# Attention scores in halves of 288 keys, with the high-by-high product on two halves of TensorE's rows

## The chip, the cores and the metric

The kernel runs on one core of a Trainium2 chip. What counts is the device time of one execution in microseconds (us); the median of three runs is given beside their lowest and highest.

## What is computed

Attention with a learned bias on relative positions for 4 batches, 8 heads, 576 positions and 64 values a head, then a mixture of 8 experts on its output, whose gate is balanced in 8 rounds of row and column sums. The change stands in the scores of the attention:

```python
scores = scale * np.matmul(q, k.transpose(0, 1, 3, 2))      # 4 x 8 heads, 576 x 576
bias = np.maximum(x @ w1 + b1, 0.0) @ w2                    # x from relative positions
scores = scores + bias.transpose(2, 0, 1)[None]
scores = scores - np.max(scores, axis=-1, keepdims=True)
attn = np.exp(scores)
attn = attn / (np.sum(attn, axis=-1, keepdims=True) + 1e-09)
out = np.matmul(attn, v)                                     # then experts: relu(x @ w1[e]) @ w2[e]
```

Inputs are float32. The kernel splits each operand into a high and a low float16 part and adds the products of parts that matter.

## The kernel before

**Stages.** Up to about 150 us the bias tables are built, expert by expert weights are loaded and the largest values of q, k and v are found. The attention runs beside this from 67 us and alone with expert 0 from about 205 to 490 us. Then come the gate, the rest of expert 0 and, to the end, experts 1 to 7.

**Units and tiles.** A unit is a pair of heads of one batch, 16 in all. `u_trans` (line 747) turns the parts of q and k so that the 64 values of a head lie on partitions: 18 transposes on TensorE into the PSUM tile `l`, and three copies out of it into `qkT`, the first and third on ScalarE, the second (k) on VectorE. `qkT` holds for q and for k the high part on partitions 0 to 63 and the low part on 64 to 127. Two copies on GpSimd (`pairs`, line 727) then make a third block in which q's low part is on partitions 0 to 63 and its high part on 64 to 127.

**Scores.** `scores` (line 898) makes one tile of 128 queries by 576 keys in the PSUM tile `s`, which spans two banks of 512 columns. For both blocks of q (as stored, and turned) it multiplies all 128 partitions with 512 keys and then with 64 keys: high by high plus low by low from the first, low by high plus high by low from the second. That is four matmuls a tile. For t = 4 the tile takes 64 queries of each of the two heads, one head on each half of the output partitions, and has eight matmuls of half the width. There are 9 tiles a unit, 144 in all. The keys stand in the order that the bias tables were built for.

**After the scores.** `st_max` (line 922) adds the bias and finds the row's extreme in one VectorE pass (`sb`, a custom operation that reads `s`); ScalarE takes the exponential, VectorE the reciprocal, ScalarE and VectorE write the high and low part `ah`, a transfer on SyncE's queue turns it into `aT` (line 981), and `attend` (line 983) multiplies with v into the tile `pv`, one head on each half of the output partitions; one pair of its 14 pairs of matmuls has only 64 partitions of input.

**What sets the order.** All of this is recorded as nodes with a cost and sorted by a planner (`Plan.emit`, line 131): each engine takes, of the nodes whose inputs are ready by the estimated times, the one of highest urgency. The cost of a TensorE node is given by `cost` (line 227): for an output of over 64 partitions, at least 64 or the width, divided by 2350, in us. Matmuls of expert 0 are nodes of the lowest urgency (`run_piece`, line 868); they fill TensorE between scores and `pv` groups and write the PSUM tile `l` too. A step is two tiles (or the one tile of t = 4), 5 steps a unit; the scores of a step are recorded one step ahead, and `u_trans` of unit u (from the fourth on) at step 5u - 4, its first scores at 5u - 1. All recorded instructions carry line 211, so the trace is read by tile names.

Of the kernel before, what the change touches and what calls it, by code (L numbers as in the profile page):

```python
# [18 lines left out]
P = 128  # L19
B, H, S, D = 4, 8, 576, 64  # L20
# [5 lines left out]
R = S // 64  # L26
# [163 lines left out]
class Engine:  # L190
# [36 lines left out]
    def cost(self, op, out, ins):  # L227

        n = max(x.free_size() for x in [out] + ins)
        columns = sum(x.free_size() == 1 for x in ins)  # L230
        if self.name == "pe":
            c = 4 if ins[0].dtype == F32 else 1
            if out.partition_size() > 64:
                return c * max(64, out.free_size()) / 2350
            return c * max(82, out.free_size()) / 3500
        if self.name == "act":
            return (0.13 if ins and ins[0].space == PSUM else 0.16) + 0.03 * columns + n * 0.00097
        if self.name == "pool":
            return 0.15 + n * 0.0016
        if op == "tensor_copy" and ins[0].dtype == out.dtype == F16:  # L240
            return 0.06 + n * 0.00027
        if n <= 2:
            return 0.08
        return 0.12 + n * (0.0012 if ins[0].space != PSUM else 0.00112)
# [27 lines left out]
def attention_sinkhorn_moe(ctx, tc, q, k, v, w1, b1, w2, wg, m1, m2, xm, xm4, xf, sel, out):  # L272
# [141 lines left out]
    with ExitStack() as actx:  # L414
# [105 lines left out]
        for kind in range(1, 4):  # L520
            vec.scalar_tensor_tensor(
                out=wr,
# [101 lines left out]
        def bias_step(between=()):  # L624
# [33 lines left out]
            out=w2m,  # L658
# [68 lines left out]
        def pairs(o, i):  # L727
            pool.tensor_copy(o.bitcast(U32), i.bitcast(U32))
# [18 lines left out]
        def u_trans(u):  # L747
            if u >= len(units):
                return
            st = U[u]  # L750
            if u in (2, 3):
                qkT = xc[:, u - 2, : 27 * P].rearrange("p (n x) -> p n x", x=P)
            else:
                qkT = uni.tile([P, 27, P], F16, name="qkT", tag="qkT")
            qk = st.pop("qk").rearrange("p (i r) a d -> p i r (a d)", i=2)
            for i in range(3):
                ps = psA.tile([P, 1024], F16, name="ps_t", tag="l1", bufs=2).rearrange("p (r x) -> p r x", x=P)
                rows = [(i, r) for r in range(8)] if i < 2 else [(0, 8), (1, 8)]
                with plan.as_one():
                    for j, (a, r) in enumerate(rows):  # L760
                        pe.transpose(ps[:, j], qk[:, a, r], id16)
                if i == 0:
                    act.copy(
                        qkT[:, 0:8].rearrange("p (h t) (i x) -> p h t i x", h=2, i=2),
                        ps.rearrange("p (i t) (h x) -> p h t i x", i=2, h=2),
                    )
                elif i == 1:
                    vec.tensor_copy(qkT[:, R : R + 8], ps)
                else:
                    act.copy(qkT[:, : 2 * R].rearrange("p (i r) x -> p i r x", i=2)[:, :, 8], ps[:, 0:2])  # L770
            for i in range(2):
                pairs(qkT[64 * i : 64 * i + 64, 2 * R :], qkT[64 - 64 * i : 128 - 64 * i, :R])
            kv = qkT[:, R : 2 * R + 1].rearrange("p (r c) x -> p c r x", r=2)
            st.update(q=(qkT[:, :R], qkT[:, 2 * R :]), kT=qkT[:, R : 2 * R], kv=kv)

        def b_load(u, hh):

# [7 lines left out]
        def b_tile(u, t, hh):  # L785
            if t in (2, 3):
                return U[u]["b", hh][:, t - 2, :]
            hp = units[u][1]
            return br[t][:, 2 * hp + hh, :] if t < 2 else br4[:, hp, :]
# [107 lines left out]

        def scores(u, t, hh):
            ps = ps_s()
            kT = U[u]["kT"]  # L900
            kv = U[u]["kv"]
            for a, qT in enumerate(U[u]["q"]):
                for c in range(2):
                    for h in (hh,) if t < 4 else (0, 1):
                        hs = slice(h * 64, h * 64 + 64)
                        lhs = qT[:, 4 * h + t, :] if t < 4 else qT[:, 8, hs]
                        rhs = kT[:, 4, hs] if c else kv[:, :4, :, hs]
                        o = (ps if t < 4 else ps[hs])[:, 512 * c : 512 + 64 * c]
                        pe.matmul(o, lhs, rhs, start=(a == 0), stop=(a == 1))
            return ps  # L910

# [10 lines left out]
        def st_max(s):  # L922
            u, gi, hh = s["key"]
            st = wrk.tile([P, 4, 2], F32, name="st", tag="st", bufs=5)
            s["st"], s["sb"] = st, []
            for i, t in enumerate(s["ts"]):
                sb = wrk.tile([P, S], F32, name="sb", tag="sb", bufs=6)
                s["sb"].append(sb)
                vec.tensor_tensor_reduce(
                    out=sb,  # L930
                    in0=s["ps"][i][:, :S],
                    in1=b_tile(u, t, hh),
                    scale=nc8[:, 0:1],
                    scalar=3.0e38,
                    op0=ALU.add,
                    op1=ALU.min,
                    accum_out=st[:, 0, i : i + 1],
                )
# [1058 lines left out]
```

## Time and profile before

| | us |
|---|---|
| median of three runs | 1743.61 (1743.52 to 1743.78) |
| the profiled execution | 1743.0 |
| its span, first to last instruction | 1741.2 |
| mean granted clock of TensorE | 0.984 |

The profile is of one execution. Engines: PE is TensorE's matmuls, PEld its weight loads, DVE VectorE, ACT ScalarE, POOL GpSimd, SP SyncE. A matmul's row gives start and length; matmuls overlap, so the spacing of starts tells the rate and not the length. `128*64` behind the tiles is the used part of the array, rows by columns. A busy share over the whole span mixes stages with different limits, so it is read by stage.

### The profile page before, as it was taken

How to read it: one execution, taken by the hardware profiler on the slowest of the kernel's cores; microseconds unless marked ns; L12 is line 12 of the kernel's file. 1: busy time of each engine (PE TensorE's matmuls, PEld its weight loads, DVE VectorE, ACT ScalarE, POOL GpSimd, SP SyncE). 2: the span in 40 equal slices, each digit the busy share in tenths (PEclk: the TensorE clock that was granted, in tenths of full speed). 3: DMA queues.
4: the chain of work that ended last, by engine and by line, in shares of the span. 5: the costliest groups of instructions: out<-in, count | busy, mean ns of one | idle time of the engine just before them, and what ended most of it. 6: DMA issues, size and time to landing. Idle time of an engine off the chain costs nothing.

```text
span 1741.2 us, 40333 instructions
## 1 busy us (share of the span) xinstructions
PE 1667.7 (96%) x16596; PEld 1368.3 (79%) x16596; DVE 1440.8 (83%) x2622; ACT 1070.2 (61%) x1906; POOL 96.8 (6%) x137
## 2 busy tenths in 40 slices
PE   7887897999999999999999999999999999999998
PEld 4554564656585888888988898889888888888887
DVE  7998989898869999787878887988788878876666
ACT  7897888888857655456455545555555644443443
POOL 0102011111002310000000000000000000000000
PEclk9988898999999999999999999999999999999999
DMA  7869899999976446734664555456544743463321
GB/s 256 257 172 235 190 211 208 215 203 208 185 228 212 148 164 230 247 145 147 218 231 170 174 187 212 173 177 237 208 163 158 281 155 133 181 224 99 102 76 37
DMA packets 291965, 324.61 MB, mean 186 GB/s; under 512 B 183100, under 2 KB 217412, under 8 KB 286788
## 3 DMA queue, kind: packets, MB, share of 16 engines
q1 hardware_dynamic: 291780, 322.04, 61.0%
q8 instruction: 129, 2.11, 0.5%
q14 instruction: 56, 0.46, 0.1%
HBM read 191.43 MB, written 88.08 MB: 161 GB/s over the span
## 4 chain that ended last, share of the span: by engine, by line
PE 81%; DVE 9%; DMA 4%; ACT 3%; issue 2%; POOL 0%; SPq 0%; DVEq 0%; ACTq 0%; POOLq 0%
PE bankA L1608 18%; PE bankA L1628 14%; PE bankE L1628 9%; PE bankB L1628 9%; PE bankE L1608 9%; PE l L211 7%; PE s L211 5%; PE bankB L1608 4%; PE pv L211 3%; DMA aT<-ah 2%; ACT area L211 1%; DVE area L211 1%; DVE ah L211 1%; DMA aT<-xc 1%; PE bankB L375 1%
## 5 line engine op out<-in xcount | busy, mean ns | idle before, releaser
L1608 PEld LDWEIGHTS <-slot 128*128 128x128 f16 x5040 | 451.0, 98 | 51.1 <-issue 5.3
L1628 PEld LDWEIGHTS <-hA 128*128 128x128 f16 x2268 | 221.0, 98 | 26.6 <-DVE hA L1220 1.2
L211 PEld LDWEIGHTS <-area 128*128 128x128 f16 (+1 forms) x2477 | 153.8, 100 | 102.8 <-issue 33.1
L1608 PE MATMUL bankA<-xt,slot 128*128 128x256 f16 (+1 forms) x1680 | 186.1, 262 | 0.7 <-ACT u L1665 0.7
L1608 PE MATMUL bankE<-xt,slot 128*128 128x256 f16 (+1 forms) x1680 | 186.1, 262 | 0.3 <-DVE c L1220 0.3
L1653 ACT ACTIVATE hA<-c 128x512 f16<-128x512 f32 x189 | 118.3, 628 | 108.5 <-DVE c L1220 107.5
L1628 PEld LDWEIGHTS <-hS 128*128 128x128 f16 x1512 | 147.5, 98 | 20.2 <-DVE hS L1659 1.9
L1628 PEld LDWEIGHTS <-area 128*128 128x128 f16 x1512 | 147.7, 98 | 17.1
L1712 ACT COPY u<-bankA 128x512 f32<-128x512 f32 (+1 forms) x70 | 37.9, 541 | 178.9 <-PE bankA L1628 178.8
L1220 DVE SCALAR_TENSOR_TENSOR hA<-c,hA 128x512 f16<-128x512 f32 x189 | 128.3, 690 | 16.0 <-ACT hA L1653 13.9
L1665 ACT ACTIVATE u<-bankA 128x512 f32<-128x512 f32 x126 | 75.1, 596 | 79.0 <-PE bankA L1608 71.9
L211 PE MATMUL l<-area 128*128 128x512 f16 (+1 forms) x413 | 110.0, 384 | 5.5 <-ACT area L211 1.3
L211 ACT ACTIVATE sb<-sb,st 128x576 f32<-128x576 f32 x144 | 110.6, 770 | 7.1 <-DVE st L211 6.8
L1220 DVE SCALAR_TENSOR_TENSOR acc<-c,fs,acc 128x256 f32<-128x256 f32 x252 | 110.3, 479 | 2.0
L211 DVE SCALAR_TENSOR_TENSOR ah<-sb,st,ah 128x576 f16<-128x576 f32 x121 | 97.5, 828 | 13.4 <-ACT ah L211 13.4
L211 PE MATMUL s<-qkT 128*128 128x512 f16 (+3 forms) x560 | 83.0, 297 | 15.5 <-DVE st L211 14.4
L211 ACT ACTIVATE ah<-sb,st 128x576 f16<-128x576 f32 x121 | 89.4, 771 | 11.6 <-DMA aT<-ah 9.6
L1628 PE MATMUL bankA<-area,hS 128*128 128x256 f16 x756 | 88.9, 273 | 1.8 <-ACT hS L1653 1.0
L1628 PE MATMUL bankA<-area,hA 128*128 128x256 f16 x756 | 88.4, 273 | 1.0 <-DVE hA L1220 1.0
L1628 PE MATMUL bankB<-area 128*128 128x256 f16 x756 | 88.3, 273 | 0.0
L1628 PE MATMUL bankB<-area,hA 128*128 128x256 f16 x756 | 88.3, 273 | 0.0
L1628 PE MATMUL bankA<-area 128*128 128x256 f16 x756 | 88.3, 273 | 0.0
(248 smaller groups left out, 3166.7 us busy)
## 6 DMA issues: line engine op xcount, KB each, us to landing
sc_w<-stage SPq DMA_DIRECT2D x84, 512.0 KB
acc<-sc_y SPq DMA_DIRECT2D x102, 256.0 KB
area<-sc_w SPq DMA_DIRECT2D x48, 512.0 KB
sc_y<-acc SPq DMA_DIRECT2D x84, 256.0 KB
xt<-sc_t SPq DMA_DIRECT2D x20, 1024.0 KB
slot<-sc_w SPq DMA_DIRECT2D x36, 512.0 KB
bt<-sc_bias SPq DMA_DIRECT2D x26, 576.0 KB
raw<-in_moe_w_dram SPq DMA_DIRECT2D x28, 512.0 KB
```

Of the source, the lines that this page charges most:

```text
L211: self.plan.record(self.name, cost, lambda: fn(*args, **kw), ins, outs, move)
L375: pe.matmul(ps, w[:, a, ft * P : (ft + 1) * P], xs(xp, dt, p0, W), start=(dt == 0 and j == 0), stop=(dt == 3 and j == 2),)
L1220: vec.scalar_tensor_tensor(out=o, in0=x, scalar=s, in1=y, op0=op0, op1=op1)
L1608: pe.matmul(ps[:, jf * w : jf * w + w], t[:, a, c * 512 + f * P : c * 512 + f * P + P], x(xp, c), start=(first and jf == 0 and c == 0 and ...
L1628: pe.matmul(ps[:, j * 256 : j * 256 + 256], h[:, a, fc * w + j * P : fc * w + j * P + P], t[:, wp, fc * 256 : fc * 256 + 256], start=(firs ...
L1653: on_act(0.58, lambda: act.activation(h[:, 0, sl], x, AF.Relu if relu else AF.Copy), [r], wk)
L1665: on_act(0.55, lambda: act.activation(tmp[k], bank[b], f, scale=HS), [b], [k], 0)
L1712: on_act(0.27 * nt, lambda: act.copy(tmp[k][:, :n], bank[b][:, :n]), [b], [k], 0)
```

## The change

`qkT` keeps its size and is laid out by head: for each head the 576 queries, and likewise the 576 keys, stand in one run (`qH`, `kH`, `zH` are views of the three blocks, two heads by 576). The copies out of `l` write in this layout. A third copy on GpSimd puts the high part of the last 288 keys of k over q's low part on partitions 64 to 127, once the turned block has been made from it.

A score tile then has two matmuls on all 128 partitions, from the turned block of q, with 288 keys each (low by high plus high by low), and two on 64 partitions, high by high: the first 288 keys from partitions 0 to 63, the last 288 from partitions 64 to 127. The product low by low is left out. Each half of the keys has a PSUM bank of its own, and VectorE's pass reads two runs of 288. The planner prices a matmul whose input has 64 partitions at its width divided by 4000.

```diff
--- before.py
+++ after.py
@@ -231,7 +231,7 @@
         if self.name == "pe":
             c = 4 if ins[0].dtype == F32 else 1
             if out.partition_size() > 64:
-                return c * max(64, out.free_size()) / 2350
+                return c * max(64, out.free_size()) / (4000 if ins[0].partition_size() == 64 else 2350)
             return c * max(82, out.free_size()) / 3500
         if self.name == "act":
             return (0.13 if ins and ins[0].space == PSUM else 0.16) + 0.03 * columns + n * 0.00097
@@ -752,26 +752,39 @@
                 qkT = xc[:, u - 2, : 27 * P].rearrange("p (n x) -> p n x", x=P)
             else:
                 qkT = uni.tile([P, 27, P], F16, name="qkT", tag="qkT")
+            qH, kH, zH = (
+                qkT[:, R * i : R * i + R].rearrange("p r x -> p (r x)").rearrange("p (h s) -> p h s", h=2)
+                for i in range(3)
+            )
             qk = st.pop("qk").rearrange("p (i r) a d -> p i r (a d)", i=2)
             for i in range(3):
                 ps = psA.tile([P, 1024], F16, name="ps_t", tag="l1", bufs=2).rearrange("p (r x) -> p r x", x=P)
-                rows = [(i, r) for r in range(8)] if i < 2 else [(0, 8), (1, 8)]
+                rows = [(0, r) for r in range(8)] if i == 0 else [(1, r) for r in (0, 5, 1, 6, 2, 7, 3, 8)]
+                if i == 2:
+                    rows = [(0, 8), (1, 4)]
                 with plan.as_one():
                     for j, (a, r) in enumerate(rows):
                         pe.transpose(ps[:, j], qk[:, a, r], id16)
                 if i == 0:
                     act.copy(
-                        qkT[:, 0:8].rearrange("p (h t) (i x) -> p h t i x", h=2, i=2),
+                        qH[:, :, : 8 * D].rearrange("p h (t i x) -> p h t i x", t=4, i=2),
                         ps.rearrange("p (i t) (h x) -> p h t i x", i=2, h=2),
                     )
                 elif i == 1:
-                    vec.tensor_copy(qkT[:, R : R + 8], ps)
+                    vec.tensor_copy(
+                        kH[:, :, : 8 * D].rearrange("p h (r x) -> p r h x", r=8),
+                        ps.rearrange("p r (h x) -> p r h x", h=2),
+                    )
                 else:
-                    act.copy(qkT[:, : 2 * R].rearrange("p (i r) x -> p i r x", i=2)[:, :, 8], ps[:, 0:2])
+                    act.copy(
+                        qkT[:, : 2 * R].rearrange("p (i r) x -> p i (r x)", i=2)
+                        .rearrange("p i (h s) -> p i h s", h=2)[:, :, :, 8 * D :],
+                        ps[:, 0:2].rearrange("p i (h x) -> p i h x", h=2),
+                    )
             for i in range(2):
                 pairs(qkT[64 * i : 64 * i + 64, 2 * R :], qkT[64 - 64 * i : 128 - 64 * i, :R])
-            kv = qkT[:, R : 2 * R + 1].rearrange("p (r c) x -> p c r x", r=2)
-            st.update(q=(qkT[:, :R], qkT[:, 2 * R :]), kT=qkT[:, R : 2 * R], kv=kv)
+            pairs(qH[64:P, :, S // 2 :], kH[0:64, :, S // 2 :])
+            st.update(q=(zH, (qH[0:64], zH[64:P])), k=(kH, (kH[0:64], qH[64:P])))
 
         def b_load(u, hh):
 
@@ -897,15 +910,14 @@
 
         def scores(u, t, hh):
             ps = ps_s()
-            kT = U[u]["kT"]
-            kv = U[u]["kv"]
-            for a, qT in enumerate(U[u]["q"]):
+            (qa, qb), (ka, kb) = U[u]["q"], U[u]["k"]
+            for a in range(2):
                 for c in range(2):
                     for h in (hh,) if t < 4 else (0, 1):
-                        hs = slice(h * 64, h * 64 + 64)
-                        lhs = qT[:, 4 * h + t, :] if t < 4 else qT[:, 8, hs]
-                        rhs = kT[:, 4, hs] if c else kv[:, :4, :, hs]
-                        o = (ps if t < 4 else ps[hs])[:, 512 * c : 512 + 64 * c]
+                        o = (ps if t < 4 else ps[h * 64 : h * 64 + 64])[:, 512 * c : 512 * c + S // 2]
+                        qT, kT = (qb[c], kb[c]) if a else (qa, ka)
+                        lhs = qT[:, h, P * t : min(P * t + P, S)]
+                        rhs = kT[:, h, S // 2 * c : S // 2 * c + S // 2]
                         pe.matmul(o, lhs, rhs, start=(a == 0), stop=(a == 1))
             return ps
 
@@ -927,9 +939,9 @@
                 sb = wrk.tile([P, S], F32, name="sb", tag="sb", bufs=6)
                 s["sb"].append(sb)
                 vec.tensor_tensor_reduce(
-                    out=sb,
-                    in0=s["ps"][i][:, :S],
-                    in1=b_tile(u, t, hh),
+                    out=sb.rearrange("p (a s) -> p a s", a=2),
+                    in0=s["ps"][i].rearrange("p (a s) -> p a s", a=2)[:, :, : S // 2],
+                    in1=b_tile(u, t, hh).rearrange("p (a s) -> p a s", a=2),
                     scale=nc8[:, 0:1],
                     scalar=3.0e38,
                     op0=ALU.add,
```

On TensorE, at the first score tile of the program (`qkT` is the turned parts of q and k, `s` the score tile, `l` the target of the transposes):

```order
 L211 MATMUL l_1_115<-id_68,qk_126 128x128
 L211 LDWEIGHTS qkT_127
-L211 MATMUL s_117<-qkT_127 128x512
+L211 MATMUL s_117<-qkT_127 128x288
 L211 LDWEIGHTS qkT_127
-L211 MATMUL s_117<-qkT_127 128x64
+L211 MATMUL s_117<-qkT_127 128x288
```

The two further matmuls of the tile change in the same way; the last two of the four are those of 64 partitions, which the order does not name. The wait for GpSimd's copies moves from the third weight load of the tile to the first, and the fourth matmul waits for the third copy.

On GpSimd, at the first units' copies within `qkT` (and `xc`, where two units keep theirs):

```order
 L211 COPY qkT_127<-qkT_127 64x576 x2
+L211 COPY qkT_127<-qkT_127 64x2x144
 L211 COPY qkT_129<-qkT_129 64x576 x2
+L211 COPY qkT_129<-qkT_129 64x2x144
 L211 COPY xc<-xc 64x576 x2
+L211 COPY xc<-xc 64x2x144
```

One copy a unit is added behind the two.

On VectorE, in the stretch where the bias still runs beside the first steps (`ISA` on `sb` is the pass over the scores, `area` and `aT_0` the bias, `ah` the low part of the weights):

```order
 L211 SCALAR_TENSOR_TENSOR vs_145<-vnat_116,sms,vs_145 128x640
+L211 ISA sb_134,st_143<-s_117,br_110,sms 128x576
+L211 ISA st_143 128x1
 L211 TENSOR_TENSOR aT_0_118<-s_119,area 128x512
-L211 ISA sb_134,st_143<-s_117,br_110,sms 128x576
-L211 ISA st_143 128x1
-L211 SCALAR_TENSOR_TENSOR area<-s_119,sms,aT_0_118 128x8x32
 L211 SCALAR_TENSOR_TENSOR qk_126<-nat_121,sms,qk_126 128x9x64
```

The planner sets the pass over a score tile ahead of a bias row; on TensorE it likewise sets fillers to other places between score tiles and `pv` groups.

## Rows read from the trace of the kernel before

**Rows 1.** The page, busy time, share of the span, instructions of each engine.
```profile
PE 1667.7 (96%) x16596; PEld 1368.3 (79%) x16596; DVE 1440.8 (83%) x2622; ACT 1070.2 (61%) x1906; POOL 96.8 (6%) x137
```

**Rows 2.** Stretches of the whole span; columns named in the first line.
```profile
core 0: us, PE busy (x) PEld busy (x) DVE busy (x) ACT busy (x) POOL busy (x), PEclk, DMA share, GB/s
...
205.00:490.00 285.00, 263.58 (x2649) 170.13 (x2644) 247.37 (x572) 241.82 (x495) 36.93 (x57) 0.98 0.98 204
...
740.00:1741.00 1001.00, 993.18 (x9561) 892.46 (x9558) 792.89 (x1288) 512.98 (x846) 0.00 (x0) 1.00 0.48 169
```

**Rows 3.** The chain of waits by line, 205 to 490 us, then 67 to 205 us.
```profile
by line: PE l L211 38.3%; PE pv L211 16.8%; PE s L211 12.0%; issue 5.8%; DMA aT<-xc 5.8%; DMA aT<-ah 4.0%; DVE ah L211 3.6%; DVE sb L211 3.3%; ACT ah L211 2.6%; DMA bt<-sc_bias 1.2%; DMA sc_y<-ys 1.0%; DVE qk L211 0.8%; DVE st L211 0.7%; DV
...
by line: PE s L211 24.8%; DMA aT<-ah 10.6%; DVE area L211 10.0%; ACT area L211 8.2%; issue 7.2%; DVE sms L211 6.2%; PE l L211 5.7%; PE pv L211 5.3%; DVE ah L211 4.8%; DVE sb L211 3.3%; DVE aT L211 3.0%; ACT sb L211 1.7%; DVE st L211 1.4%; A
```

**Rows 4.** TensorE in order of time, 309.0 to 315.3 us: start, length, tiles, count.
```profile
309.62 1.14 PE L211 MATMUL s<-qkT 128*128 128x512 f16 x8
310.60 1.48 PE L211 MATMUL l<-xb,area 128*128 128x256 f16 x12
311.91 0.65 PE L211 MATMUL s<-qkT 128*128 128x512 f16 x4
312.50 1.96 PE L211 MATMUL pv<-aT,vs 128*64 128x256 f16 x28
314.39 0.28 PE L211 MATMUL l<-id,qk 128*128 128x128 f16 x2
314.60 0.68 PE L211 MATMUL s<-qkT 128*64 128x512 f16 x8
315.22 0.28 PE L211 MATMUL l<-id,qk 128*128 128x128 f16 x2
```

**Rows 5.** The same view of short cuts: inside and around one `pv` group.
```profile
313.29 0.50 PE L211 MATMUL pv<-aT,vs 128*64 128x256 f16 x4
...
313.49 0.30 PE L211 MATMUL pv<-aT,vs 64*64 64x256 f16 x2
...
313.72 0.30 PE L211 MATMUL pv<-aT,vs 128*64 128x256 f16 x2
```

**Rows 6.** Transfer queues, 205 to 490 us: packets, MB, share of 16 engines.
```profile
q1 hardware_dynamic: 146436, 57.82, 97.4%
```

**Rows 7.** Who waited for whom, 205 to 490 us: total us, times, longest.
```profile
DVE sb L211 <- PE s L211: 9.0, 14, 1.2
PE s L211 <- DVE st L211: 8.7, 12, 1.6
...
PE pv L211 <- DMA aT<-xc: 4.3, 3, 3.5
```

**Rows 8.** Groups of instructions, 0 to 760 us: busy, mean ns, idle before.
```profile
L211 DVE CUSTOM_DVE_ANT_0 sb<-s,br,sms 128x576 f32<-128x576 f32 x80 | 63.6, 808 | 4.5 <-PE s L211 4.5
...
L211 DVE CUSTOM_DVE_ANT_0 sb<-s,bt,sms 128x576 f32<-128x576 f32 x64 | 51.4, 811 | 6.9 <-PE s L211 5.9
...
L211 DVE TENSOR_TENSOR aT<-s,area 128x512 f32<-128x512 f32 x40 | 27.5, 687 | 7.1 <-PE s L211 5.8
...
L211 DVE TENSOR_TENSOR area<-l,area 128x512 f16<-128x512 f32 x27 | 18.4, 684 | 6.2 <-ACT area L211 6.0
```

**Rows 9.** Tile `qkT`, whole span: duration ns min/median/max, first and last start.
```profile
L211 PE MATMUL s<-qkT x560: 190/318/637, 67.4 to 471.4; 128*128 128x64 f16 x75, 128*128 128x512 f16 x74, 128*64 128x64 f16 x20, 128*64 128x512 f16 x18
L211 ACT COPY qkT<-l x28: 348/685/1019, 62.7 to 449.7; 128x1024 f16<-128x1024 f16 x14, 128x256 f16<-128x256 f16 x14
L211 POOL COPY qkT<-qkT x28: 662/665/1198, 64.5 to 450.9; 64x576 uint32<-64x576 uint32 x28
L211 DVE COPY qkT<-l x14: 670/683/692, 63.9 to 448.9; 128x1024 f16<-128x1024 f16 x14
```

**Rows 10.** The group of score matmuls, 205 to 490 us.
```profile
L211 PE MATMUL s<-qkT 128*128 128x512 f16 (+1 forms) x480 | 68.0, 288 | 9.0 <-DVE st L211 8.7
```

**Rows 11.** A stretch at a lower granted clock; columns as in rows 2.
```profile
300.00:307.00 7.00, 3.67 (x28) 2.40 (x28) 5.78 (x12) 4.02 (x9) 0.00 (x0) 0.52 0.98 196
```

## The prediction

> **What bounds the kernel now.** I read the busy times first [rows 1], then the same by stage [rows 2], then the chain of waits of the two attention stretches [rows 3], then TensorE's instructions in order of time where the changed work stands [rows 4, 5]. TensorE is busy 96% of the span, but the change touches only the attention, which ends near 490 us; from 740 us on TensorE is busy 993.18 of 1001 us and nothing there changes. In the steady attention, 205 to 490 us, no engine is alone: TensorE 263.58 of 285 us, VectorE 247.37, ScalarE 241.82, and the transfer queue's packets took 97.4% of 16 engines' span [rows 2, 6]. The chain settles which of them is late most often: `l`, `pv` and `s` on TensorE are 38.3 + 16.8 + 12.0 = 67.1% of it, transfers of `aT` 9.8%, VectorE's two largest lines 6.9%. In 67 to 205 us, where the bias still runs, TensorE's three are 24.8 + 5.7 + 5.3 = 35.8% [rows 3]. So two thirds of what TensorE gains or loses per score tile after 205 us should arrive at the end, and about a third before. What TensorE waits for there is small and scattered: 8.7 us for `st` on VectorE, 4.3 us for a transposed `aT` [rows 7].
>
> **Columns saved.** A score tile streams 512 + 64 + 512 + 64 = 1152 columns. Two tiles start at 309.62 and the next work at 310.60, so one takes 0.49 us [rows 4]. Twelve matmuls of 256 columns go from 310.60 to 311.91, 0.109 us each, so one of 288 columns takes 0.109 x 288 / 256 = 0.123 us. The new tile has two of them on all 128 rows (0.245 us) and two on 64 rows. If those two run side by side they cost one, 0.123 us; that two matmuls on different parts of the array can do so is seen for the two column halves: a `pv` group has 28 matmuls of 256 columns and takes 1.89 us, where 28 one after the other would be 3.05 [rows 4]. For two row halves no row shows it. Side by side, a tile streams 0.368 us: 0.12 us saved, and 144 tiles (80 against `br`, 64 against `bt` [rows 8]) save 17.7 us of TensorE. One after the other, nothing is saved, since 4 x 288 is again 1152.
>
> **Switches added.** The price that the diff does not show is the change between matmuls that use the whole array and matmuls that use a part. It is in the trace of before, at every `pv` group. The stretch from 311.91 to 314.39 holds one score tile (0.49 us), 14 pairs (14 x 0.109 = 1.53 us) and the switches into the group, to the 64-row pair inside it, back, and out: 2.48 - 2.02 = 0.46 us for four, 0.116 us each [rows 4]. The same in single starts: pairs that otherwise follow at 0.11 us stand 0.20 us ahead of the 64x64 pair (313.29 to 313.49) and 0.23 us behind it (313.49 to 313.72) [rows 5]. That pair differs from its neighbours in rows alone, which makes it the nearest row to a change from 128 to 64 rows. With 128 columns at this type no row shows such a change; the two ends for its price are 0 (nothing drains) and 0.14 us (0.23 of the way back, less 0.09), and I take 0.116. The Trainium skill, page TensorEngine Tiling (Array Packing), section Key Properties, says that a change of tiling mode, and not of the tile alone, drains the engine; the rows just named agree, and by that rule the price stands for 64x128 too.
>
> Counted in the order of the built programs, TensorE changes its form 110 times outside the `pv` groups before and 372 times after: each of the 144 tiles has one switch more inside, and one more behind it unless a `pv` group follows at once. 262 x 0.116 = 30.4 us added against 17.7 saved: TensorE has 12.7 us more to do, 0.09 us a tile. A whole-array tile amid other whole-array work goes from 0.49 to 0.368 + 0.232 = 0.60 us; a tile before a `pv` group, and the t = 4 tile, which stands between two switches already (0.62 us from 314.60 to 315.22 [rows 4]), stay as they are.
>
> **The other parts.** Row copies: VectorE's copy of k writes runs of 64 in place of one run of 1024. It took 0.683 us, ScalarE's copies of such runs up to 1.019 [rows 9]; so 0 to 0.34 us on each of 16, at most 5.4 us on an engine whose two largest lines are 6.9% of the chain, under 0.5 us at the end. A gain is excluded, the elements being the same. I take 0. VectorE's pass over the scores reads two runs of 288; reading PSUM in runs of 32 (the bias, 687 ns for 512) costs what reading it in one run does (684 ns for 512, the fillers) [rows 8], so 0, and 144 x 0.003 = 0.4 us either way as bound. GpSimd gets one copy more a unit, of half the elements of one of 0.665 us: 16 x 0.33 to 0.67. It is busy 36.93 of 285 us [rows 2]; the first score matmul now waits for it, but the transposes are issued three steps ahead of a unit's first scores (about 14 us at 60 steps in 285 us), and the list of waits of before has no score matmul behind GpSimd [rows 7]. If that cover were gone it would cost 0.7 us a unit, 11 us in all. Only unit 0 is near: its copies start at 64.5, its scores at 67.4 [rows 9]; 0.4 us there, in a stretch where TensorE is a third of the chain. I take 0. What queues behind a late score on TensorE is the next filler or `pv` group, and what queues behind its `sb` on VectorE is the low part of the step before, whose transpose the transfer queue waits for.
>
> **The order.** The planner's price of a tile falls from 0.49 to 0.389 us while the tile by my sum rises to 0.60, so it sees room that is not there and sets expert-0 matmuls (the `l` fillers) earlier: around the 13th to 15th `pv` group up to 24 matmuls of 256 columns (2.6 us) earlier, elsewhere the same or within 12. The total is the same. Bounds for this: 2.6 us either way; I take 0.
>
> **The sum.** 12.7 us over 144 tiles. After 205 us stand 480 score matmuls [rows 10], 12 units of 40, which is 108 tiles: 9.5 us x 0.67 = 6.4 us; 36 tiles before: 3.2 x 0.36 = 1.1 us. Together 7.5 us. The profiled execution took 1743.0 us with a span of 1741.2; the median of the three runs is 0.6 above it, and the sum on the median is 1743.6 + 7.5 = 1751.
>
> **Rivals.**
> *The switch by rows alone is nearly free and the halves do run side by side.* Then 17.7 us are saved: 13.3 x 0.67 + 4.4 x 0.36 = 10.5 us less, 1733 us. For it: no row shows 128 to 64 rows at 128 columns. Against it: the 64x64 pair of [rows 5]. It decides when a switch costs under 17.7 / 262 = 0.068 us. The Trainium skill, page TensorEngine Tiling (Array Packing), section Theoretical Speedup, gives up to 2x for a side of at most 64 and charges nothing in that place, which is this case; the trace has the drain beside the gain at every `pv` group.
> *The halves run one after the other.* Each tile streams as before and the switches are all on top: 22.8 x 0.67 + 7.6 x 0.36 = 18.0 us, 1762 us. For it: no row has two row halves at work. Against it: the column halves.
> *Absorbed.* The transfers, not TensorE, set the pace from 205 to 490 us, and the added 9.5 us fill waits that TensorE has anyway (the 13 us of [rows 7] named above); then 0 to 3 us arrive, 1745 us. For it: 97.4% [rows 6]; against it: 67% against 9.8% of the chain.
> A further risk goes one way: where TensorE stood idle, its granted clock fell to its lower level, as in 300 to 307 us (0.52, with TensorE busy 3.67 of 7 us) [rows 11]. One more such stretch costs at most 3.5 us, half of its length.
>
> **Chances.** Forecast as summed (1746 to 1758) 0.54; one after the other (1758 to 1770) 0.10; absorbed (1740 to 1746) 0.22; free switches or a lucky order (1730 to 1740) 0.14. The range leaves out the last and the upper part of the second: 1740 to 1764. A difference of 0.2%, 3.5 us, is about what a measurement of this kernel can tell from none: faster 0.14, same 0.22, slower 0.64.
>
> **What would show it.** In the profile after: a score tile amid `l` work from 0.49 to about 0.60 us, its last two starts within 10 ns of each other (0.12 us apart if they queue), about 0.2 us in place of 0.12 between the second and the third start, and 0.2 us from the last start to the next whole-array matmul. TensorE's work from 205 to 490 us would stretch by some 6 us, and the stage from 740 us on would keep its length. The forecast is wrong if the third start follows the second at 0.13 us (no switch), or if the tile takes 0.60 us and the attention still ends at 490 us (absorbed).

## The result and the profile after

The changed kernel takes 1758.74 us (median of 4 runs, 1755.04 to 1759.57); the kernel before, run beside it, takes 1743.69 (1743.52 to 1743.81). The ratio is 1.0083, with an interval of 1.0068 to 1.0098. A second set of runs gave 1753.56 (5 runs, 1753.27 to 1757.39) and 1.0064 (1.0051 to 1.0076). So the change costs 0.6 to 0.8%, 11 to 15 us. I had forecast 7.5 us, with a range up to 20: slower, as forecast, and one and a half to two times as much of it. The experiments ask where the rest comes from.

The profiled execution took 1759.57 us, its span 1757.6. First the page of the changed kernel, the busy time of TensorE as in [rows 1]:

```profile
PE 1683.4 (96%) x16596; PEld 1365.0 (78%) x16596; DVE 1442.1 (82%) x2622; ACT 1070.2 (61%) x1906; POOL 105.6 (6%) x153
```

TensorE is busy 15.7 us longer with as many matmuls; VectorE and ScalarE do what they did, and GpSimd has 16 copies more (8.8 us). Where the attention ends is seen at the first matmul of the routing after it. Before, in order of time (start, length, what, tiles, count):

```profile
492.58 1.36 PE L1276 MATMUL bankS<-wgs,xa 128*128 128x8 f16 x48
```

After, the same row:

```profile
508.81 1.36 PE L1288 MATMUL bankS<-wgs,xa 128*128 128x8 f16 x48
```

It starts 16.23 us later. From there to the last matmul the two executions take 1244.5 and 1244.6 us, and each kernel run below 1243.2 to 1245.5. So the whole loss lies in the attention, and this one row tells how late a profiled execution is.

**A score tile after**, TensorE in order of time, to be laid beside [rows 4]; then the same kernel in short cuts, whose starts give the single matmuls:

```profile
332.85 0.64 PE L211 MATMUL s<-qkT 128*128 128x288 f16 x4
333.42 1.48 PE L211 MATMUL l<-xb,area 128*128 128x256 f16 x12
...
324.29 0.64 PE L211 MATMUL s<-qkT 128*128 128x288 f16 x4
324.86 0.41 PE L211 MATMUL pv<-aT,vs 128*64 128x256 f16 x4
```

```profile
332.97 0.52 PE L211 MATMUL s<-qkT 128*128 128x288 f16 x3
...
333.19 0.30 PE L211 MATMUL s<-qkT 64*128 64x288 f16 x2
333.42 0.28 PE L211 MATMUL l<-xb,area 128*128 128x256 f16 x1
```

The four starts are 332.85, 332.97, 333.19 and 333.19 (3 ns apart by the records' own times): the two halves run side by side. The third start is 0.22 us behind the second, where a matmul of 288 columns alone takes 0.123, and the next whole-array matmul 0.23 behind the pair. So a switch (the change between matmuls that use the whole array and matmuls that use 64 rows) costs about 0.10 us each way, and a tile amid whole-array work takes 0.57 us against 0.49 before. Ahead of a `pv` group (324.29 to 324.86) it takes 0.57 against 0.59 in [rows 4].

**The stages and the chain.** The stretch of [rows 2], 205 to 490 us, and the chain of waits from 205 us to the end of the attention, as in [rows 3]:

```profile
205.00:490.00 285.00, 265.08 (x2573) 160.67 (x2572) 242.77 (x563) 236.47 (x483) 44.47 (x72) 0.94 0.92 194
```

```profile
by line: PE l L211 46.9%; PE pv L211 19.1%; PE s L211 15.2%; issue 4.2%; DVE ah L211 2.8%; DVE sb L211 2.1%; DMA aT<-xc 1.8%; ACT ah L211 1.3%; ACT xc L211 0.8%; ACT sb L211 0.8%; DVE qk L211 0.8%; DVE area L211 0.7%; DVE st L211 0.6%; DVE 
```

TensorE's three lines rise from 67.1 to 81.2% of the chain, and transfers of `aT` fall from 9.8 to about 2%: VectorE, ScalarE and the transfers wait more for TensorE than before. In the list of waits, where the columns are total us, times and longest, two rows grew against [rows 7]:

```profile
DVE sb L211 <- PE s L211: 15.5, 18, 1.8
PE s L211 <- DVE st L211: 9.0, 10, 1.7
...
PE l L211 <- DVE qk L211: 6.8, 3, 2.8
...
PE s L211 <- POOL qkT L211: 0.2, 1, 0.2
```

VectorE waits for scores 15.5 us instead of 9.0. The wait of `l` (here the transposes of q and k) for VectorE's `qk` was a single one before, of 2.7 us, and is now three with 6.8. The one that I had weighed, scores behind GpSimd's copy, is 0.2 us in all. That extra wait for `qk` has nothing to do with a switch. It is a sign that TensorE's order is another.

### The profile page after: what moved, and what is told of

Its sections match the earlier page's. It is cut to its first block, busy times and chain, and to the rows that moved or that the text cites. A ratio compares the mean times of both kernels' runs of the same rounds, so it can differ in the third digit from the quotient of the medians.

```text
span 1757.6 us, 40416 instructions
## 1 busy us (share of the span) xinstructions
PE 1683.4 (96%) x16596; PEld 1365.0 (78%) x16596; DVE 1442.1 (82%) x2622; ACT 1070.2 (61%) x1906; POOL 105.6 (6%) x153
## 4 chain that ended last, share of the span: by engine, by line
PE 85%; DVE 9%; ACT 3%; issue 2%; DMA 2%; POOL 0%; SPq 0%; DVEq 0%; ACTq 0%; POOLq 0%
PE bankA L1620 18%; PE bankA L1640 14%; PE bankE L1640 9%; PE l L211 9%; PE bankB L1640 9%; PE bankE L1620 9%; PE s L211 5%; PE bankB L1620 4%; PE pv L211 4%; DVE area L211 1%; DVE sms L211 1%; ACT area L211 1%; DVE ah L211 1%; PE bankB L375 1%; DVE sb L211 1%
## 5 line engine op out<-in xcount | busy, mean ns | idle before, releaser
L211 PE MATMUL s<-qkT 128*128 128x288 f16 (+3 forms) x560 | 85.8, 309 | 13.7 <-DVE st L211 12.5
```

Of the source, the lines that this page charges most:

```text
L211: self.plan.record(self.name, cost, lambda: fn(*args, **kw), ins, outs, move)
```

## The experiments

Four things are mixed in the change: the layout (two banks, rows of 64), the halves side by side, the switches, and the order in which the planner lays TensorE's work, since the change also lowers the price of a tile there from 0.49 to 0.389 us while the tile really takes 0.57. My theory at the start: the layout and the order are nothing, the switches all. The rival: the order is worth as much as the switches.

**The price alone put back.** TensorE's order is then that of before in all but 16 of its 16,567 places, and the work is that of the change:

```diff
-                return c * max(64, out.free_size()) / (4000 if ins[0].partition_size() == 64 else 2350)
+                return c * max(64, out.free_size()) / 2350
```

> The change with one line taken back: the planner prices a 64-row matmul as every other (2350), so TensorE's order is that of before again, with the new score tiles in it. Theory 1 (the switches between 128 and 64 rows are the loss): TensorE still has 370 switches outside the pv groups against 110, about 0.09 us more a tile, so the time stays at 1752 to 1760 us. Rival 2 (the planner's lower price moved the fillers to wrong places, and that is the loss): 1742 to 1747 us.

Measured: 1748.87 us, ratio 1.0035 (1.0022 to 1.0047). About half of the loss is gone (from 1.0064 or 1.0083), with every switch in place. Its trace can be read beside that of before place by place (`...` in these extracts stands for rows left out). TensorE of this kernel in order of time; the second to fifth row answer to the first four of [rows 4]:

```profile
283.78 2.62 PE L211 MATMUL pv<-aT,vs 128*64 128x256 f16 x20
...
310.77 1.22 PE L211 MATMUL s<-qkT 128*128 128x288 f16 x8
311.92 1.48 PE L211 MATMUL l<-xb,area 128*128 128x256 f16 x12
313.24 0.64 PE L211 MATMUL s<-qkT 128*128 128x288 f16 x4
313.80 1.96 PE L211 MATMUL pv<-aT,vs 128*64 128x256 f16 x28
...
498.15 1.36 PE L1288 MATMUL bankS<-wgs,xa 128*128 128x8 f16 x48
```

In the execution before, the `pv` row stood at 283.79 too; two tiles took 0.98 us (here 311.92 - 310.77 = 1.15), and the attention ends at 498.15 where it ended at 492.58. So 5.6 us are lost in this execution, and none of them up to 284 us. Its mean granted clock is 0.978 where before has 0.984, but the loss doesn't hang on that: two other executions of this kernel, at 0.984 and 0.983, took 1748.78 and 1749.72 us.

**The layout alone.** Both products on all 128 rows, with the two banks, the copies in runs of 64 and the old price. The low by low products come back with it, as before:

```diff
-            pairs(qH[64:P, :, S // 2 :], kH[0:64, :, S // 2 :])
-            st.update(q=(zH, (qH[0:64], zH[64:P])), k=(kH, (kH[0:64], qH[64:P])))
+            st.update(q=(zH, (qH, qH)), k=(kH, (kH, kH)))
```

> The new layout, the halves of 288 keys and the two PSUM banks, but high by high (with low by low again) on all 128 rows, no third copy on GpSimd, and the old price: no row halves and no added switch. Theory 1: a tile is 4 x 0.122 = 0.49 us as before and the time is that of before, 1741 to 1747 us. Rival 3 (the copies in runs of 64 and VectorE's pass over two runs are the loss): 1750 us or more, with VectorE's copy or its score pass longer in the profile.

Measured: 1743.25 us, 1.0006 (0.9997 to 1.0015): nothing that can be told from the kernel before. TensorE's order is exactly that of before, four matmuls of 288 columns take what 512 + 64 did, and VectorE's pass keeps its 808 ns. In time order, a tile in this kernel, and its pass over the scores (busy us, mean ns, idle before):

```profile
373.17 0.65 PE L211 MATMUL s<-qkT 128*128 128x288 f16 x4
373.66 0.61 PE L211 MATMUL l<-id,qk 128*128 128x128 f16 x8
```

```profile
L211 DVE CUSTOM_DVE_ANT_0 sb<-s,br,sms 128x576 f32<-128x576 f32 x80 | 63.7, 808 | 5.0 <-PE s L211 4.8
```

**The halves on the same rows**, so that they can't run side by side, with everything else as in the change:

```diff
-            pairs(qH[64:P, :, S // 2 :], kH[0:64, :, S // 2 :])
-            st.update(q=(zH, (qH[0:64], zH[64:P])), k=(kH, (kH[0:64], qH[64:P])))
+            st.update(q=(zH, (qH[0:64], qH[0:64])), k=(kH, (kH[0:64], kH[0:64])))
```

> The change, but both halves of the keys on rows 0 to 63, so that the two 64-row matmuls of a tile have to follow each other; no third copy on GpSimd; price and switches as in the change. Theory 1 (in the change the halves run side by side): 0.12 us more a tile, 17.7 us more of TensorE, of which two thirds or more arrive: 1770 to 1778 us. Rival 4 (the halves queue in the change already): the time of the change, 1755 to 1760 us.

Measured: 1768.41 us, 1.0146 (1.013 to 1.0161). The tile, in time order:

```profile
385.62 0.76 PE L211 MATMUL s<-qkT 128*128 128x288 f16 x4
386.31 0.94 PE L211 MATMUL l<-xb,area 128*128 128x256 f16 x7
```

0.69 us, 0.12 more than in the change: what running side by side saves is a whole matmul of 288 columns.

**The order of that kernel without its work.** The layout kernel, whose tile takes 0.49 us, told that a tile takes 0.389. TensorE's order is the one of the kernel just above:

```diff
                     s["ps"].append(scores(u, t, hh))
+                    plan.group[1] = 0.3891 if t < 4 else 0.6583
```

> The kernel of e2 (all score matmuls on 128 rows, no third copy) with the change's price alone: a tile's node is set to 0.389 us (t = 4: 0.658), so that the planner orders nearly as in the change while a tile takes 0.49 us and no switch is added. Rival 2 in its strong form (the order itself costs, whatever the tile): 1749 to 1755 us. Its weak form (the order costs only where the tile is longer than the planner believes, by 0.1 us here against 0.19 in the change): 1743 to 1748 us. No effect of the price: 1741 to 1745 us.

Measured: 1748.67 us, 1.0017 (1.0006 to 1.0027). No switch is added, no column is saved, and 3 us are lost: the order is not nothing. It also prices the switches a second time. Same order, 0.49 against 0.69 us a tile: 1.0146 - 1.0017 = 0.0129, 22 us. With 0.20 us on the 118 tiles that have two switches more and about 0.1 on the other 26 (those ahead of a `pv` group and most with t = 4), TensorE has some 26 us more; so about 85% of it arrived.

**As large an error as the change makes.** The change's planner is wrong by 0.57 - 0.389 = 0.18 us a tile, the last kernel's only by 0.10. So the layout kernel again, with 0.30 for a tile of 0.49, and its opposite, a price too high by 0.09:

```diff
                     s["ps"].append(scores(u, t, hh))
+                    plan.group[1] = 0.30 if t < 4 else 0.56
```

> e2 (all score matmuls on 128 rows, a tile of 0.49 us) with a tile priced at 0.30 us (t = 4: 0.56), so that the planner is wrong by 0.19 us a tile, as it is in the change by 0.389 against 0.58. No switch is added. If the size of the error is what the order costs: 1750 to 1758 us. If the error alone does little and it takes the switches beside it: 1743 to 1750 us.

```diff
                     s["ps"].append(scores(u, t, hh))
+                    plan.group[1] = 0.58 if t < 4 else 0.658
```

> e2 with a tile priced at 0.58 us (t = 4: 0.658), 0.09 us too dear, which is the order of e7 but for some rows. If every order other than that of before costs some us: 1747 to 1752 us. If only a price that is too low costs: 1742 to 1746 us.

Measured: 1752.73 us, 1.0042 (1.0026 to 1.0058), and 1746.4 us, 1.0019 (1.001 to 1.0028). The error of the change's size costs 7 us with no switch at all; added to the 1.0035 of the switches it gives 1.0077, between the two ratios of the change. A price too high costs 3 us too, so what decides is not the sign of the error. Of the orders tried with the layout kernel's work, that of the old price has the lowest ratio, though the interval of 1.0006 reaches into those of 1.0017 and 1.0019.

Where these losses arise is read from the starts of VectorE's 144 passes over the scores. Against the layout kernel, which has the order of before and no switch, the k-th pass of a profiled execution starts later by so many us:

```
pass                      37     55     67    103    139
layout kernel, at      215.2  262.8  286.6  374.1  461.5
old price (switches)    -1.3    0.0    0.8    5.6    6.4
wrong price (order)      7.3    4.8   13.2   13.3   13.5
the change               6.1    3.2   12.9   14.4   16.9
the change once more     2.4   -0.5    7.2    9.7   10.9
old price, pair turned   2.2    3.3    3.6    6.3    6.9
smaller wrong price      0.4    0.9    2.5    7.8    6.7
```

("Wrong price" is the kernel with 0.30; its profiled execution took 1756.61 us, about 4 above its median. "Pair turned" is the old price's order with fewer switches, described below; "smaller wrong price" is the kernel with 0.389.) By the same measure the kernel before stands 0.4 to 1.6 us behind the layout kernel. In the first four rows the two causes seem to lie in different stretches: the switches cost little up to pass 67 and some 6 us behind it, the order costs up to pass 67 and nothing behind, and the change has both. The last two rows show that this is no rule. With the pair turned, half of the loss is there by pass 67. The smaller wrong price loses 5.3 us from pass 67 to 103, 3.9 of them from pass 95 on (352 to 374 us); from 350 to 376 us its granted clock is 0.87 where before has 1.00.

Up to pass 37 the loss is not steady: 6.1 us and 2.4 for one and the same kernel. From pass 37 to 67 it is: 5.9 us with the wrong price, 6.8 and 4.8 in the change, of which the kernel with the old price accounts for 2.1 by its switches. What TensorE's program holds there, counted in the order of the built programs: matmuls of expert 0 (in units of 256 columns), `pv` matmuls and transposes of q and k that stand ahead of the n-th of the 640 score matmuls, 4.4 to a pass:

```
score matmul   before, old price    the change       wrong price
170  (pass 38)   132  321  102     132  321  102    132  321  102
220  (pass 50)   228  405  112     252  405  112    240  405  112
250  (pass 56)   336  489  146     336  461  130    336  461  130
260  (pass 58)   360  489  146     336  489  138    336  489  138
280  (pass 63)   384  517  148     384  517  148    384  517  148
```

At both ends the same work has been done. Between them up to 24 matmuls of expert 0 come ahead of scores, as I had read from the order, and a `pv` group of 28, 16 transposes and 24 matmuls of expert 0 fall behind scores, which I had not. The scores are early then (the dip at pass 55), and what was put behind them is late. In the order of the smaller wrong price the `pv` group stands where it did and only 8 transposes fall behind (138 ahead of the 250th score matmul); from pass 37 to 67 that kernel lost 2.1 us. The link from these pieces to the loss is read from order and trace; no run moves them alone. The transposes start the next unit, and behind them TensorE has nothing to lay into a wait: in every one of these kernels about 36 us follow without a matmul of expert 0 (272.0 to 308.3 us before, 283.0 to 320.5 in the change). There TensorE stands waiting for VectorE. TensorE of the change, 289 to 316 us, with the idle time ahead of a row and its releaser in brackets:

```profile
289.20 1.94 PE L211 MATMUL s<-qkT 128*128 128x288 f16 x8 [1.07 <-DVE st L211]
293.34 1.89 PE L211 MATMUL l<-id,qk 128*128 128x128 f16 x16 [2.20 <-DVE qk L211]
295.16 3.48 PE L211 MATMUL pv<-aT,vs 128*64 128x256 f16 x28
...
310.62 1.37 PE L211 MATMUL s<-qkT 128*128 128x288 f16 x8 [1.72 <-DVE st L211]
314.76 1.04 PE L211 MATMUL l<-id,qk 128*128 128x128 f16 x8 [2.77 <-DVE qk L211]
315.72 3.48 PE L211 MATMUL pv<-aT,vs 128*64 128x256 f16 x28
```

The wrong-price kernel, without a switch, waits at the same two steps:

```profile
293.43 1.89 PE L211 MATMUL l<-id,qk 128*128 128x128 f16 x16 [2.08 <-DVE qk L211]
...
313.61 1.03 PE L211 MATMUL l<-id,qk 128*128 128x128 f16 x8 [2.28 <-DVE qk L211]
```

The kernel before has one such wait in its stretch, at 281.97, and the one with the old price too; their later one there is for a transposed `aT`:

```profile
281.97 1.03 PE L211 MATMUL l<-id,qk 128*128 128x128 f16 x8 [2.75 <-DVE qk L211]
...
303.33 3.42 PE L211 MATMUL pv<-aT,vs 128*64 128x256 f16 x27 [3.48 <-DMA aT<-xc]
```

So the waits of this stretch are no longer in the change than before (its idle times sum to 10.1 us, before to 11.8); the change comes to them later. The 28 matmuls of a `pv` group take 3.48 us there and 1.96 elsewhere: behind such waits the granted clock is for a time at the lower of its two levels (1.2 and 2.4 GHz). From 284 to 320 us its mean is 0.87 before, 0.72 in the change, 0.76 with the wrong price and 0.71 with the old price. Some of what is lost in these executions is lost that way; how much, no run separates.

```profile
284.00:320.00 36.00, 27.82 (x300) 17.91 (x297) 31.54 (x75) 29.36 (x61) 5.41 (x9) 0.87 0.96 201
...
284.00:320.00 36.00, 25.78 (x245) 14.36 (x244) 30.00 (x70) 28.93 (x61) 6.64 (x12) 0.72 0.93 197
```

(The first row is the kernel before, the second the change, with the columns of [rows 2].) VectorE and the transfers are starved ahead of these waits: 205 to 284 us with the columns of [rows 2], for the kernel before, then for the change, then for the wrong price:

```profile
205.00:284.00 79.00, 73.06 (x730) 46.05 (x726) 71.10 (x163) 68.92 (x142) 11.46 (x17) 0.97 0.97 206
```

```profile
205.00:284.00 79.00, 75.67 (x710) 44.60 (x708) 65.12 (x151) 61.99 (x125) 11.41 (x18) 0.94 0.86 183
```

```profile
205.00:284.00 79.00, 74.95 (x735) 50.42 (x734) 67.01 (x154) 63.87 (x131) 8.27 (x12) 0.96 0.88 186
```

TensorE is the busier one, by 2 to 3 us (part of that may be its clock, 0.94 and 0.96 against 0.97), and VectorE does 4 to 6 us less, with the transfers down from 0.97 to 0.86 and 0.88. With the old price that row reads 69.90 us for VectorE and 0.96, though its switches are all there.

**The true price with the change's work.** If the error is the fault, the right figure should mend it:

```diff
                     s["ps"].append(scores(u, t, hh))
+                    plan.group[1] = 0.58 if t < 4 else 0.658
```

> The change with the tile's node set to what the profile of the change shows, 0.58 us. If the wrong price was the loss, an order made with the right one is at least as good as e1's: 1745 to 1749 us. If any order other than that of before costs some us: 1752 to 1758 us.

Measured: 1750.31 us, 1.0022 (1.0012 to 1.0032). That is less than the change loses and no more than the old price does (1.0035, the intervals overlap). How the 1.0022 is shared is not shown. The layout kernel with the same prices has this order but for 192 places and loses 1.0019 with no switch, so by this pair the switches cost 0.0003, 0.5 us, with some 2.3 us of uncertainty either way, where the old price's order has them at 6 (1.0035).

**Fewer switches.** In every second tile the 64-row pair goes first, so that two tiles in a row share a form: 331 switches outside `pv` groups where the change has 372 and before had 110. Once with the change's price, once with the old one:

```diff
-            for a in range(2):
+            odd = t in (1, 3)
+            for a in (1, 0) if odd else (0, 1):
...
-                        pe.matmul(o, lhs, rhs, start=(a == 0), stop=(a == 1))
+                        pe.matmul(o, lhs, rhs, start=(a == int(odd)), stop=(a != int(odd)))
```

> The change with the same order of nodes, but in the second tile of each step the 64-row matmuls come first, so that two tiles that stand next to each other share a switch: 331 switches outside the pv groups in place of 372. Theory 1: 41 x 0.1 us = 4 us less on TensorE, 1753 to 1757 us. Rival 2 (the order, not the switches): the time of the change within 1.5 us, 1757 to 1760 us.

> e1 and e4 together: the old price, and in the second tile of a step the 64-row matmuls first: 333 switches outside the pv groups in place of 370 in e1. Theory 1: 37 x 0.1 us = 3.7 us less on TensorE than e1, most of it after 250 us: 1745 to 1748 us. If the switches that fall away were hidden: as e1, 1747 to 1750 us.

Measured: 1756.45 us, 1.0077 (1.0057 to 1.0097), and 1748.14 us, 1.0027 (1.0015 to 1.0039). Against the change (1.0064 and 1.0083) and the old price (1.0035) that is no difference that the intervals tell apart. About 40 switches of 0.1 us are 4 us of TensorE, and an interval is 4 to 7 us wide: inconclusive.

**Both tiles of a step in one piece**, with the second tile turned as above, which brings the switches down to 257:

```diff
-            def one(t):
+            def both():
                 with plan.as_one():
-                    s["ps"].append(scores(u, t, hh))
+                    for t in s["ts"]:
+                        s["ps"].append(scores(u, t, hh))
+                    plan.group[1] = 0.94 if len(s["ts"]) == 2 else 0.658
 
-            return [lambda t=t: one(t) for t in s["ts"]]
+            return [both]
```

> The two tiles of a step as one node (priced 0.94 us), the second turned, so that each pair has one run of 64-row matmuls: 257 switches outside the pv groups, 147 more than before, 14.7 us against 17.7 us of columns saved. Theory 1 by TensorE's sum alone: 3 us less than before, 1740 to 1744 us. If the order decides (a pair holds TensorE for 0.94 us at once, and VectorE gets its first tile no earlier): 1746 to 1756 us.

Measured: 1762.32 us, 1.0098 (1.0079 to 1.0116): a clear miss. The list of waits of this kernel from 205 us on has two rows that hardly exist before:

```profile
PE pv L211 <- DMA aT<-ah: 7.1, 4, 2.5
PE l L211 <- DVE area L211: 6.5, 5, 3.7
```

So the order changed again, and for the worse. Which part of it is at fault (the second tile's later scores, or the fillers that go elsewhere) was not settled.

**More of the same load.** The old price's kernel with the 64-row work of a tile cut in two, one piece ahead of the whole-array pair and one behind it. That makes one switch more and one small pair more a tile, with the order of the tiles unchanged:

```diff
+                for part in ("first", "full", "second"):
+                    for c in range(2):
+                        x, y = (qa, ka) if part == "full" else (qb[c], kb[c])
+                        at, n = (w if part == "second" else 0), (2 * w if part == "full" else w)
```

> e1 (the change in the order of before) with the switches of a whole tile doubled and no column added: the first 144 columns of each 64-row product come ahead of the two whole-array matmuls, the second 144 behind them, six matmuls a tile in place of four, at the same price for the planner. 128 tiles x 2 switches x about 0.1 us = 25.6 us more of TensorE than e1. Theory 1 (switches are what is paid, and two thirds or more arrive after 205 us): 14 to 22 us more than e1, 1762 to 1771 us. If switches were mostly hidden by other waits: under 1756 us.

Measured: 1762.68 us, 1.011 (1.0096 to 1.0124). The tile, in time order:

```profile
380.49 0.76 PE L211 MATMUL s<-qkT 64*128 64x144 f16 x6
381.18 1.48 PE L211 MATMUL l<-xb,area 128*128 128x256 f16 x12
382.60 1.34 PE L211 MATMUL s<-qkT 64*128 64x144 f16 x12
383.87 1.48 PE L211 MATMUL l<-xb,area 128*128 128x256 f16 x12
```

A tile by itself takes 0.69 us from its first start, and has a switch ahead of that, so some 0.22 us more than a tile of the change. Two tiles in a row take 383.87 - 382.60 = 1.27 us and one switch ahead, against 1.15, so again 0.22 us more for both: the second begins in the form in which the first ends. A tile behind a `pv` group has the switch ahead of it already. Counted in the order of the built programs, this kernel has 146 switches more than the one with the old price, not the 256 that I had expected. At 0.11 us each (0.22 for two) that is some 16 us of TensorE; 0.0075 of 1744, 13 us, arrived, about 80%.

**The change once more**, beside the last three:

> The change once more, on the chip of these runs and in as many rounds: the interaction of order and switches is the gap between it and e1 (1.0035 times before). If the gap is real: 1.006 to 1.010 times before. If it came from the chip: 1.003 to 1.005.

Measured: 1753.56 us, 1.0064 (1.0051 to 1.0076). None of these kernels is faster than the one before.

## Why the prediction was right, and where it was off

*The sign and the place* held: TensorE is the bound in the attention, and nothing behind it changed its length. That the time fell into the range is in part luck: the first median, 1758.74 us, lies in the band that I had given to "one after the other" (1758 to 1770), which did not happen, and the range reaches that far for this rival.

*Columns saved* held. The halves run side by side (3 ns apart), and with the same rows for both the tile is 0.12 us longer. The rival "one after the other" fell on this.

*The switch price* was 0.116 us by the `pv` groups; the new switch from 128 to 64 rows took about 0.10 each way, so the nearest row was the right one to take. (The upper end of its price takes off 0.09 us where pairs follow at 0.11; it should read 0.12 and not 0.14, which changes nothing behind it.) The tile is 0.57 us where I had 0.60. TensorE's net addition comes to 0.08 x 118 - 0.02 x 26, about 9 us, instead of 12.7. The rival of a nearly free switch (under 0.068 us) fell. The rule of the Trainium skill, page TensorEngine Tiling (Array Packing), section Key Properties, that a change of tiling mode drains the engine, agrees with these 0.10 us; the same page's "Up to 2×" in Theoretical Speedup is there for the pair, and a whole tile still got longer.

*The shares* were 7.5 of 12.7, or 0.59, and somewhat low. With order held, 6 of 9 us arrived (old price against before; 4 to 8 by the interval), 22 of 26 (same rows against its order alone) and 13 of 16 (double load); only the pair with the right price, 1.0022 against 1.0019, has next to none. "Absorbed" fell: the kernel with the old price is slower by more than its interval. The split by stage is open: I had a third arrive before 205 us and two thirds behind it. In the profiled execution with the old price nothing arrived up to pass 67 (286 us) and 5.6 us for the 77 passes that were left; with the pair turned, at the same price, 3.6 had arrived by pass 67 and 6.9 by pass 139.

*The other parts* held: copies, VectorE's pass, banks together 1.0006 (0.9997 to 1.0015), and scores wait 0.2 us in all for GpSimd. VectorE's copy of k went from 683 to 691 ns.

*The order* is the term that failed. I had seen that the planner takes 0.389 for a tile of 0.60 and sets fillers up to 2.6 us earlier. I priced that as work moved with the total unchanged, 0 with 2.6 us either way. That bound holds only for the fillers' own time, and I had looked only at them: a `pv` group and the transposes of the next unit moved the other way, into a stretch where no filler is left to cover a delay. With no switch it cost about 7 us (1.0042, 1.0026 to 1.0058) at the change's error and 3 us (1.0017) at the change's price. So the sum should have read about 6 for the switches and 3 to 7 for the order, 9 to 13; measured were 15 and 10.

That the loss has these two parts is shown, by kernels that have the one without the other. How large the order's part is in the change itself is not: none of the kernels without a switch has the change's order place by place (of the 16,567 places, 408 differ with the price of 0.30 and 314 with 0.389; in the kernel before it is 724). That the parts add up exactly is not shown either: 1.0035 + 0.0042 against 1.0064 and 1.0083, each with some 0.0013 to 0.0016 of uncertainty.

## What to carry to other kernels

Before work is split into forms that use part of the array, price the switch from a place in the trace where the form changes already. Here a pair of half-height matmuls saves 0.12 us and needs two switches of 0.10, so by this sum it can pay only if several pairs share them, or where a switch stands anyway. The kernels here that shared switches did not come out faster than the one before. When a planner or a cost table sets the order, give it the measured cost of the new work or keep the old figure, and measure an order-only kernel beside the work-only one: a wrong price of 0.2 us on 144 nodes cost as much as the slower work itself. Work that is moved can cost what it delays, and not only its own length.

## What was not expected of the hardware

Two matmuls on different halves of the rows, into two banks, start 3 ns apart, without a wait between them.

The granted clock differs between executions of one and the same kernel, and its time with it: the changed kernel took 1759.57 and 1759.3 us at mean clocks of 0.974 and 0.977, and 1755.04 at 0.983; in the second set its profiled execution took 1753.27 at 0.983. About 4 to 5 us of the 16 that the profiled pair differs by go along with that clock; whether the edit or chance lowered it, no run separates. That may be why the first ratio is the higher of the two. At like clocks the loss and its two parts are still there: the change took 1753.27 us at 0.983 where before, beside it, took 1742.85 to 1745.54; the wrong price 1746.64 and 1747.88 at 0.985 where before took 1740.22 to 1745.02; and the old price 1748.78 at 0.984 where before took 1741.99 to 1747.02. So some 9, 5 and 5 us remain at a like clock.
